# Message arithmetic in place in PSUM, with ScalarE making the bfloat16 parts, and VectorE taking them early in the step

## The chip, the cores and the metric

The kernel runs on one core of a Trainium2 chip. The metric is the device time of one execution in microseconds (us). The engines are named as in the profile: PE is TensorE's matmul, PEld its weight load, DVE is VectorE, ACT is ScalarE, POOL is GpSimd, SP is SyncE. Each engine works through its own instructions in order, and semaphores hold an instruction until what it needs from another engine is done.

## The reference

A message-passing layer on a random graph with 12,500 nodes and 800,000 edges: messages are made per edge and summed per destination node.

```python
N, deg, D, De = 12500, 64, 64, max(16, 1)
E = N * deg
...
m_in = jnp.concatenate([x[src], x[dst], e_attr], axis=-1)
msg = _silu(m_in @ w_msg)
agg = _segment_sum(msg, dst, N)
return _silu(jnp.concatenate([x, agg], axis=-1) @ w_upd)
```

All tensors are float32. `src` and `dst` are random, so edges have to be brought into the order of their destinations first.

## The kernel before

Nodes are cut into buckets of 98 (`BK`). The kernel runs two pipelines in one loop.

The first sorts the edges. A step (`Step`) takes eight columns of 128 edges: `onehot` makes, on ACT, a one-hot row of the bucket for each edge (eight Square instructions at L378, one Relu over all at L379); `sums` adds these up on DVE (L387 to L392, the first slice copied by ACT at L385); `count` forms counts on PE (L405 to L408); `ranks` reduces them on DVE (L413); `expand` writes the records to the places of their ranks (L422 to L426, DVE); `move` gathers them into the buckets with PE (L441), and ACT copies a finished chunk out of PSUM (L445). `place` computes new write pointers (L458, L459) and `scatter` writes the chunk to a store in HBM with an indirect DMA, issued by POOL (L463).

The second works through the sorted store. A group (`Group`) forms over several steps (`fourth`, `middle`, `fifth`) and loads 64 tiles of 128 edges; a batch (`Batch`) is eight of these tiles. `gather` fetches the source nodes' rows with eight indirect DMAs on POOL (L623). `onehot` makes q, the one-hot of the destination within the bucket, on DVE (L628), and ACT copies the edge features beside it (L629). `transpose` turns q with PE (L637), and ACT copies the result to qt (L640), after copying the weights w (L616). `product` multiplies qt with the weights into the PSUM bank pre (L646). `message` adds the gathered rows (DVE, L652) and applies Silu (ACT, L653). `parts` splits the float32 message into three bfloat16 parts by two subtractions (DVE, L661): the upper half of each float32 word is the part, and the rest goes on to the next. `reduce` multiplies the parts with q's one-hot (PE, L672), and `add` sums the parts (L685) and adds them to the accumulator (L687).

The tiles of a bucket come in units of one, two and, for most of the run, four (`QU`); only batches with units of four are split into parts, the others go through a float32 matmul (L674).

`period` writes out by hand the order in which one round of both pipelines is issued. In it h is the step that is new, z the one before, p and s older ones; q is the batch that is new, t the one before, a the one before that, and r the oldest. The order on each engine is that of the calls. PSUM banks, like pre, tq and z, have one buffer each; messages have two, gathered rows three, the buckets' one-hots (hf) three.

Of the kernel before, what the change touches and what calls it, by code (L numbers as in the profile page):

```python
# [17 lines left out]
D = 64  # L18
# [26 lines left out]
def mpnn_kernel(tc, x, e_attr, src, dst, w_msg, w_upd, out):  # L45
# [22 lines left out]
    with es:  # L68
# [294 lines left out]
        class Step:  # L363
# [10 lines left out]
            def onehot(c):  # L374
                c.hf = hp.tile([P, M, NBK], F32, name="hf")

                for k in range(M):
                    nc.scalar.activation(c.hf[:, k, :], iof, AF.Square, bias=c.hi[:, k:k + 1])  # L378
                nc.scalar.activation(c.hf, c.hf, AF.Relu, bias=ones, scale=-1.0)  # L379
# [216 lines left out]
        class Batch:  # L596
# [51 lines left out]
            def message(t):  # L648
                w = t.n * D
                t.msg = mp.tile([P, 3, BT * D], F32, name="msg")  # L650
                u_ = t.msg[:, 2, :]
                nc.vector.tensor_tensor(out=u_[:, 0:w], in0=t.pre[:, 0:w], in1=t.g.rearrange("p a b -> p (a b)")[:, 0:w], op=OP.add)  # L652
                nc.scalar.activation(t.msg[:, 0, 0:w], u_[:, 0:w], AF.Silu)  # L653

            def parts(t):

                t.split = t.grp.u == QU
                if t.split:
                    up = t.msg.bitcast(BF16).rearrange("p k (f two) -> p k f two", two=2)
                    for k in range(2):  # L660
                        nc.vector.tensor_tensor(out=t.msg[:, k + 1, :], in0=t.msg[:, k, :], in1=up[:, k, :, 1], op=OP.subtract)  # L661

            def reduce(t):
                t.ag = pag.tile([P, 512], F32, name="ag")
                w = 3 * D
                if t.split:
                    q = t.q.bitcast(BF16).rearrange("p i (k two) -> p i k two", two=2)[:, :, 0:BK, 1]
                    m = t.msg.bitcast(BF16).rearrange("p k (f two) -> p k f two", two=2)[:, :, :, 1]
                for i in range(t.n):
                    u, k = i // t.grp.u, i % t.grp.u  # L670
                    if t.split:
                        nc.tensor.matmul(t.ag[0:BK, u * w:(u + 1) * w].rearrange("p (k d) -> p k d", d=D), q[:, i, :], m[:, :, i * D:(i + 1) * D], start=(k == 0), stop=(k == t.grp.u - 1))  # L672
                    else:
                        nc.tensor.matmul(t.ag[0:BK, u * D:(u + 1) * D], t.q[:, i, 0:BK], t.msg[:, 0, i * D:(i + 1) * D], start=(k == 0), stop=(k == t.grp.u - 1))  # L674
# [17 lines left out]
        def period(step=None, batch=None, ptr_new=None):  # L692
# [12 lines left out]
            if h:  # L705
                h.onehot()
            if q:
                q.onehot()
            for g in forms:
                g.fourth()  # L710
# [26 lines left out]
            if a:  # L737
# [399 lines left out]
```

## Time and profile before

| | us |
|---|---|
| median of 3 runs | 9224.63 |
| lowest and highest | 9221.28, 9232.15 |
| the profiled execution | 9227.92 |
| its span | 9226.0 |

| engine | busy us | share of the span |
|---|---|---|
| PE | 8209.7 | 89% |
| PEld | 5889.5 | 64% |
| DVE | 8201.5 | 89% |
| ACT | 5087.3 | 55% |
| POOL | 6721.0 | 73% |

A group's row in the profile gives line, engine, operation, output and inputs by the program's names, shapes and count, then the busy time in us with the mean of one in ns, then the engine's idle time just before these instructions, and what ended it. A row of the timeline gives start and duration in us, engine, line, operation, names, and a count if several are merged. Durations of neighbours on one engine overlap a little, so the distance between two starts is what an instruction costs its queue. An issue of an indirect DMA counts as POOL's busy time; the fixed pause between two of them is listed as idle.

### The profile page before, as it was taken

The page shows a single profiled execution, that of the slowest core. Times are in us where ns is not written, and L with a number is a line of the kernel's source. Part 1 is how long each engine was busy: PE and PEld are TensorE (multiplying, and loading weights), DVE is VectorE, ACT ScalarE, POOL GpSimd, SP SyncE. Part 2 cuts the span into 40 slices and gives each one's busy share as a digit, 9 for nine tenths or more (in the row PEclk, how much of TensorE's full clock was granted, in tenths as well). Part 3 has the DMA queues.
Part 4 walks back from the last instruction along what each step waited for, and adds up shares of the span by engine and source line. Part 5 has one row for each costly group of instructions (what it writes and reads, how often), then busy time and mean ns, then how long its engine had stood idle before and what let it go on. Part 6 is the DMA issues. An engine that isn't in the chain of part 4 may idle for free. (4 is left out here: it accounts for less than half of the span.)

```text
span 9226.0 us, 146657 instructions
## 1 busy us (share of the span) xinstructions
PE 8209.7 (89%) x44136; PEld 5889.5 (64%) x44897; DVE 8201.5 (89%) x17559; ACT 5087.3 (55%) x12546; POOL 6721.0 (73%) x6868
## 2 busy tenths in 40 slices
PE   8999999898888889988888889888888888888777
PEld 4677766666666666666666666666666666666676
DVE  6999999999999999999999999999999999999332
ACT  5555556555555555555555555555555555555222
POOL 1566667777777777777777777777777777777776
PEclk9999999999999999999999999999999999999666
DMA  2222222222222222222222222222222222222333
GB/s 58 48 53 53 53 53 58 55 49 53 52 56 50 55 51 53 53 53 55 52 50 53 55 50 55 55 50 56 51 54 54 50 56 49 56 54 48 55 50 50
DMA packets 651770, 487.53 MB, mean 53 GB/s; under 512 B 475175, under 2 KB 522727, under 8 KB 650967
## 3 DMA queue, kind: packets, MB, share of 16 engines
q0 software_dynamic: 235968, 344.76, 16.8%
q1 hardware_dynamic: 412295, 132.58, 6.8%
q8 instruction: 361, 5.91, 0.3%
q14 instruction: 442, 3.62, 0.1%
q10 hardware_dynamic: 2704, 0.66, 0.1%
HBM read 330.05 MB, written 147.34 MB: 52 GB/s over the span
## 5 line engine op out<-in xcount | busy, mean ns | idle before, releaser
L623 POOL DMA_INDIRECT g<-A_d,sidx x6322 | 6182.9, 978 | 2084.3 <-issue 1561.6
L441 PE MATMUL pl<-X,hf 128*128 128x223 f32 (+5 forms) x12504 | 4191.7, 485 | 0.0
L441 PEld LDWEIGHTS pl<-X,hf 128*128 128x128 f32 x12504 | 2292.3, 190 | 1347.6 <-issue 1026.6
L426 DVE TENSOR_TENSOR X<-cb,rec 128x442 f32<-128x442 f32 (+5 forms) x3126 | 2710.3, 929 | 27.1
L378 ACT ACTIVATE hf<-iof,shi 128x128 f32<-128x128 f32 x6256 | 1910.9, 389 | 1364.8 <-PE pl L441 1361.5
L646 PEld LDWEIGHTS pre<-w,qt 114*128 114x128 f32 x10368 | 1266.3, 193 | 330.0 <-issue 313.9
L646 PE MATMUL pre<-w,qt 114*128 114x64 f32 x10368 | 1241.2, 273 | 52.0 <-DVE msg L652 49.0
L653 ACT ACTIVATE msg<-msg 128x512 f32<-128x512 f32 (+1 forms) x818 | 501.4, 613 | 1205.9 <-DVE msg L652 1202.1
L413 DVE TENSOR_REDUCE rank<-z 128x8 f32<-128x1024 f32 x782 | 950.4, 1215 | 71.0 <-PE z L408 41.4
L652 DVE TENSOR_TENSOR msg<-pre,g 128x512 f32<-128x512 f32 (+1 forms) x818 | 546.5, 668 | 492.8 <-DMA g<-A_d,sidx 348.3
L640 ACT ACTIVATE qt<-tq 114x1024 f32<-114x1024 f32 (+1 forms) x818 | 800.9, 979 | 327.6 <-PE tq L637 326.9
L406 PE MATMUL z<-G,onesb 128*128 128x384 bf16 x1564 | 515.8, 330 | 475.2 <-DVE G L387 428.6
L661 DVE TENSOR_TENSOR msg<-msg 128x512 f32<-128x512 f32 x1296 | 893.0, 689 | 22.6
L379 ACT ACTIVATE hf<-hf,ones 128x1024 f32<-128x1024 f32 x782 | 898.7, 1149 | 25.4
L637 PE MATMUL tq<-ident,q 128*114 128x128 f32 x6322 | 886.9, 286 | 14.7 <-ACT nodes L185 13.3
L637 PEld LDWEIGHTS tq<-ident,q 128*114 128x114 f32 x6322 | 781.9, 142 | 141.2 <-ACT nodes L185 21.2
L672 PE MATMUL ag<-msg,q 128*98 128x192 bf16 x5184 | 570.7, 252 | 290.5 <-DVE msg L661 111.5
L445 ACT ACTIVATE blk<-pl 128x512 f32<-128x512 f32 x521 | 309.0, 593 | 931.2 <-PE pl L441 923.3
L628 DVE TENSOR_TENSOR q<-cb,lo 128x784 f32<-128x784 f32 (+1 forms) x818 | 769.0, 940 | 0.6
L463 POOL DMA_INDIRECT st<-blk,ptrs x520 | 519.7, 999 | 338.4 <-issue 133.8
L672 PEld LDWEIGHTS <-q 128*98 128x98 bf16 x5184 | 488.6, 126 | 376.6 <-issue 324.9
L646 PEld LDWEIGHTS pre<-BW,qt 114*128 114x128 f32 x2276 | 331.7, 225 | 150.6 <-issue 149.9
(145 smaller groups left out, 6673.2 us busy)
## 6 DMA issues: line engine op xcount, KB each, us to landing
g<-A_d,sidx POOLq DMA_INDIRECT x6322
ea<-in_e_attr SPq DMA_DIRECT2D x260, 192.0 KB
rt<-st SPq DMA_DIRECT2D x1296, 34.0 KB
st<-blk,ptrs POOLq DMA_INDIRECT x520
rt<-st SPq DMA_DIRECT2D x498, 8.5 KB
nodes<-in_x SPq DMA_DIRECT2D x62, 98.0 KB
rt<-st SPq DMA_DIRECT2D x320, 17.0 KB
A_d<-nodes SPq DMA_DIRECT2D x32, 98.0 KB
```

Source lines behind the costliest of these rows:

```text
L378: nc.scalar.activation(c.hf[:, k, :], iof, AF.Square, bias=c.hi[:, k:k + 1])
L379: nc.scalar.activation(c.hf, c.hf, AF.Relu, bias=ones, scale=-1.0)
L413: nc.vector.tensor_reduce(out=c.rank, in_=c.z, axis=AX.X, op=OP.max)
L426: nc.vector.tensor_tensor(out=c.x[:, k:k + 2, 2:2 + n * R].rearrange("p k (s c) -> p k s c", c=R), in0=hit[:, k:k + 2, 0:n, None].to_broad ...
L441: nc.tensor.matmul(pl[:, 0:w], c.hf[:, k, :], c.x[:, k, 0:w], start=False, stop=(n == C - 1))
L623: nc.gpsimd.indirect_dma_start(out=t.g[:, i, :], out_offset=None, in_=A_d, in_offset=bass.IndirectOffsetOnAxis(ap=t.grp.sidx[:, k:k + 1], ...
L628: nc.vector.tensor_tensor(out=t.q[:, 0:n, 0:BK], in0=ioB[:, None, 0:BK].to_broadcast([P, n, BK]), in1=t.grp.lo[:, i0:i0 + n, None].to_broa ...
L637: nc.tensor.transpose(t.tq[0:KQ, j * P:(j + 1) * P], t.q[:, j, :], ident)
L640: nc.scalar.activation(t.qt[:, 0:w], t.tq[0:KQ, 0:w], AF.Copy)
L646: nc.tensor.matmul(t.pre[:, i * D:(i + 1) * D], t.qt[:, i * P:(i + 1) * P], w, start=True, stop=True)
L661: nc.vector.tensor_tensor(out=t.msg[:, k + 1, :], in0=t.msg[:, k, :], in1=up[:, k, :, 1], op=OP.subtract)
L672: nc.tensor.matmul(t.ag[0:BK, u * w:(u + 1) * w].rearrange("p (k d) -> p k d", d=D), q[:, i, :], m[:, :, i * D:(i + 1) * D], start=(k == 0 ...
```

## The change

A split message stays in the PSUM bank in which its product was made. DVE adds the gathered rows there, in place; ACT applies Silu there, in place, and then copies the result to a bfloat16 tile in SBUF: the first part. DVE subtracts that part from the message in PSUM, in place; ACT copies the remainder to bfloat16: the second part. DVE's second subtraction writes the third part, bfloat16, directly. The bank is free for the next product only after that. Messages that aren't split get their sum in place too, and Silu writes them to a float32 tile. The parts now lie contiguous, where they were every other bfloat16 of a float32 tile.

In `period`, the sum and Silu of batch a come before the ranks of step z, both subtractions come in the first half of the step, around the one-hot of batch q, and the eight Squares of step h are split in two halves around them. `fourth` of the forming groups moves behind the second subtraction, and `add` behind `expand`.

```diff
-            def onehot(c):
-                c.hf = hp.tile([P, M, NBK], F32, name="hf")
-
-                for k in range(M):
+            def onehot(c, part=None):
+
+                if part != 1:
+                    c.hf = hp.tile([P, M, NBK], F32, name="hf")
+
+                for k in range(0 if part != 1 else ZB, M if part != 0 else ZB):
                     nc.scalar.activation(c.hf[:, k, :], iof, AF.Square, bias=c.hi[:, k:k + 1])
-                nc.scalar.activation(c.hf, c.hf, AF.Relu, bias=ones, scale=-1.0)
+                if part != 0:
+                    nc.scalar.activation(c.hf, c.hf, AF.Relu, bias=ones, scale=-1.0)
...
             def message(t):
                 w = t.n * D
-                t.msg = mp.tile([P, 3, BT * D], F32, name="msg")
-                u_ = t.msg[:, 2, :]
-                nc.vector.tensor_tensor(out=u_[:, 0:w], in0=t.pre[:, 0:w], in1=t.g.rearrange("p a b -> p (a b)")[:, 0:w], op=OP.add)
-                nc.scalar.activation(t.msg[:, 0, 0:w], u_[:, 0:w], AF.Silu)
-
-            def parts(t):
-
                 t.split = t.grp.u == QU
+                pre = t.pre[:, 0:w]
+                nc.vector.tensor_tensor(out=pre, in0=pre, in1=t.g.rearrange("p a b -> p (a b)")[:, 0:w], op=OP.add)
                 if t.split:
-                    up = t.msg.bitcast(BF16).rearrange("p k (f two) -> p k f two", two=2)
-                    for k in range(2):
-                        nc.vector.tensor_tensor(out=t.msg[:, k + 1, :], in0=t.msg[:, k, :], in1=up[:, k, :, 1], op=OP.subtract)
+                    t.msg = mp.tile([P, 3, BT * D], BF16, name="msg")
+                    nc.scalar.activation(pre, pre, AF.Silu)
+                    nc.scalar.activation(t.msg[:, 0, 0:w], pre, AF.Copy)
+                else:
+                    t.msg = mp.tile([P, BT * D], F32, name="m32")
+                    nc.scalar.activation(t.msg[:, 0:w], pre, AF.Silu)
+
+            def part(t, k):
+
+                if t.split:
+                    nc.vector.tensor_tensor(out=t.pre if k == 1 else t.msg[:, k, :], in0=t.pre, in1=t.msg[:, k - 1, :], op=OP.subtract)
+                    if k == 1:
+                        nc.scalar.activation(t.msg[:, k, :], t.pre, AF.Copy)
...
@@ period
             if q:
                 q.gather(BT // 2, BT)
-            if h:
-                h.onehot()
-            if q:
-                q.onehot()
-            for g in forms:
-                g.fourth()
             if z:
                 z.count()
             if t:
...
                 t.transpose(1)
             if r:
                 r.reduce()
+            if a:
+                a.message()
             if z:
                 z.ranks()
+            if h:
+                h.onehot(0)
             if a:
-                a.message()
+                a.part(1)
+            if q:
+                q.onehot()
+            if h:
+                h.onehot(1)
+            if a:
+                a.part(2)
+            for g in forms:
+                g.fourth()
+            if z:
+                z.expand()
             if r:
                 r.add()
-            if z:
-                z.expand()
             if h:
                 h.sums()
...
             if e:
                 e.place(ptr_new)
-            if a:
-                a.parts()
             for g in forms:
                 g.middle()
                 g.fifth()
```

`reduce` reads the parts as `t.msg[:, :, i * D:(i + 1) * D]` in place of the strided view.

More of the change, by code (lines that the diff above doesn't have):

```diff
@@ L671, in reduce @@
                     if t.split:
[L672 removed]
+                        nc.tensor.matmul(t.ag[0:BK, u * w:(u + 1) * w].rearrange("p (k d) -> p k d", d=D), q[:, i, :], t.msg[:, :, i * D:(i + 1) * D], start=(k == 0), stop=(k == t.grp.u - 1))
                     else:
[L674 removed]
+                        nc.tensor.matmul(t.ag[0:BK, u * D:(u + 1) * D], t.q[:, i, 0:BK], t.msg[:, i * D:(i + 1) * D], start=(k == 0), stop=(k == t.grp.u - 1))
             def add(t):
```

1 line of the change is left out of this document (removed).

## The prediction

> **What bounds the kernel now.** I read the busy times by stretch first, then each engine's groups inside the long stretch, then the timeline of single steps. Columns of the first view: busy time of PE, PEld, DVE, ACT and POOL, with instruction counts, and the granted TensorE clock.
>
> ```profile
> core 0: us, PE busy (x) PEld busy (x) DVE busy (x) ACT busy (x) POOL busy (x), PEclk, DMA share, GB/s
> 0.00:1440.00 1440.00, 1368.59 (x7045) 939.06 (x7173) 1277.13 (x3103) 842.24 (x2091) 800.60 (x842) 1.00 0.24 53
> 1440.00:8520.00 7080.00, 6334.81 (x34091) 4473.92 (x34725) 6682.20 (x13789) 4078.41 (x10137) 5408.16 (x5487) 0.99 0.23 53
> 8520.00:8700.00 180.00, 119.83 (x654) 107.30 (x654) 69.75 (x186) 43.74 (x97) 131.67 (x137) 0.64 0.29 55
> 8700.00:9226.00 526.00, 386.50 (x2352) 369.26 (x2351) 172.41 (x482) 122.94 (x223) 380.59 (x405) 0.66 0.32 51
> ```
>
> Batches that split their messages (four tiles to a bucket) run in the second stretch. Its groups on POOL and DVE:
>
> ```profile
> L623 POOL DMA_INDIRECT g<-A_d,sidx x5065 | 4986.5, 984 | 1543.5 <-issue 1223.5 <-DMA g<-A_d,sidx 215.5 <-DVE q L628 47.5
> L463 POOL DMA_INDIRECT st<-blk,ptrs x422 | 422.3, 1001 | 128.6 <-issue 115.5 <-ACT blk L445 7.9 <-ACT msg L653 2.1
> ```
>
> ```profile
> L661 DVE TENSOR_TENSOR msg<-msg 128x512 f32<-128x512 f32 x1270 | 875.1, 689 | 22.1
> L413 DVE TENSOR_REDUCE rank<-z 128x8 f32<-128x1024 f32 x634 | 769.8, 1214 | 0.0
> ...
> L652 DVE TENSOR_TENSOR msg<-pre,g 128x512 f32<-128x512 f32 x634 | 435.4, 687 | 201.9 <-issue 107.9 <-DMA g<-A_d,sidx 91.1
> ...
> L423 DVE TENSOR_TENSOR cb<-cb,rank 128x240 f32<-128x240 f32 x634 | 259.1, 409 | 0.0
> ```
>
> L413 runs once a step: 634 steps in 7080 us, 11.17 us each. POOL's two groups, busy and idle, make 4986.5+1543.5+422.3+128.6 = 7081 us: POOL issues without a break, eight gathers of 0.984+0.305 us and two thirds of a scatter per step. So POOL sets the pace, by a little: DVE's only large wait is for gathers, 201.9/634 = 0.32 us, so DVE needs 11.17-0.32 = 10.85 us a step. Whatever adds over 0.32 us to DVE's step makes DVE the bound. PE is busy 6334.81/634 = 9.99 us, ACT 6.4.
>
> **The chain that the new order closes.** Call S the end of a step's last sum on DVE (L389 or L392). PE's count of the next step waits for S, the transposes follow it, then ACT's copy to qt (L640). Three steps; columns are start, duration, engine, line:
>
> ```profile
> 5013.27 0.23 DVE L392 TENSOR_TENSOR G<-G 128x128 bf16<-128x128 bf16 x1
> ...
> 5013.44 0.94 POOL L623 DMA_INDIRECT g<-A_d,sidx  x1 [0.31 <-issue]
> 5013.59 1.03 PE L637 MATMUL tq<-ident,q 128*114 128x128 f32 x8
> ...
> 5013.80 1.41 DVE L661 TENSOR_TENSOR msg<-msg 128x512 f32<-128x512 f32 x2
> ...
> 5014.66 0.29 ACT L629 ACTIVATE q<-rt 128x128 f32<-128x128 f32 x1
> 5014.68 1.35 POOL L623 DMA_INDIRECT g<-A_d,sidx  x1 [0.30 <-issue]
> 5014.86 0.38 ACT L616 ACTIVATE w<-BW 114x64 f32 x2
> 5015.13 0.21 DVE L506 CAST sidx<-rt 128x64 int32<-128x64 f32 x1
> 5015.15 1.00 ACT L640 ACTIVATE qt<-tq 114x1024 f32<-114x1024 f32 x1
> ...
> 5015.78 0.97 DVE L628 TENSOR_TENSOR q<-cb,lo 128x784 f32<-128x784 f32 x1
> ...
> 5016.66 1.22 DVE L413 TENSOR_REDUCE rank<-z 128x8 f32<-128x1024 f32 x1
> ...
> 5017.83 0.69 DVE L652 TENSOR_TENSOR msg<-pre,g 128x512 f32<-128x512 f32 x1
> ...
> 5018.44 0.55 DVE L685 TENSOR_REDUCE sum<-ag 98x128 f32<-98x384 f32 x1
> ```
>
> ```profile
> 5023.78 0.36 DVE L389 TENSOR_TENSOR G<-G,hf 128x128 bf16<-128x128 bf16 x1
> ...
> 5024.38 1.41 DVE L661 TENSOR_TENSOR msg<-msg 128x512 f32<-128x512 f32 x2
> ...
> 5034.54 0.23 DVE L392 TENSOR_TENSOR G<-G 128x128 bf16<-128x128 bf16 x1
> 5034.68 1.41 DVE L661 TENSOR_TENSOR msg<-msg 128x512 f32<-128x512 f32 x2
> ```
>
> ```profile
> 5024.58 1.03 PE L637 MATMUL tq<-ident,q 128*114 128x128 f32 x8
> ...
> 5035.23 1.04 PE L637 MATMUL tq<-ident,q 128*114 128x128 f32 x8
> ```
>
> From S to the end of the transposes: 14.62-13.50 = 1.12, 25.61-24.14 = 1.47, 36.27-34.77 = 1.50; mean 1.36 us. Today this hurts nobody: after S, DVE does the parts of the batch before, the one-hot and the ranks, and comes to the sum (L652) 4.3 us later (5017.83 against 13.50), when qt is long copied; and between a message's Silu and its parts lie the expansion and the sums of the step, so that DVE never waits for ACT there.
>
> The changed program's queues, as built, are: DVE: sum (message), ranks, part 1, one-hot q, part 2, then expansion, add, sums. ACT: w, **copy to qt**, Silu, copy 0, four squares, copy 1, the features of q, four squares, Relu, G. PE is unchanged: count, transposes, reduction, moves, product. Queues run in order. Silu itself needs only the sum, but it stands behind the qt copy, hence behind the transposes and S; and DVE waits at part 1 with everything else of the step queued behind it: q, part 2, the expansion, the sums, and so the next S. The ring S, transposes, qt, Silu, copy, parts, expansion, next S is closed, and its length is the step.
>
> Prices on ACT, from the groups of the same stretch, and eight squares from the timeline:
>
> ```profile
> L379 ACT ACTIVATE hf<-hf,ones 128x1024 f32<-128x1024 f32 x633 | 727.6, 1149 | 20.6
> L640 ACT ACTIVATE qt<-tq 114x1024 f32<-114x1024 f32 x634 | 638.9, 1008 | 175.1 <-PE tq L637 174.9
> L653 ACT ACTIVATE msg<-msg 128x512 f32<-128x512 f32 x634 | 398.6, 629 | 1019.9 <-DVE msg L652 1019.2
> L385 ACT ACTIVATE G<-hf 128x256 bf16<-128x256 f32 x633 | 253.0, 400 | 0.0
> L445 ACT ACTIVATE blk<-pl 128x512 f32<-128x512 f32 x423 | 250.5, 592 | 670.2 <-PE pl L441 669.5
> ```
>
> ```profile
> 5011.13 2.44 ACT L378 ACTIVATE hf<-iof,shi 128x128 f32<-128x128 f32 x8 [3.08 <-PE pl L441]
> ```
>
> *First stall.* From S: transposes 1.36, qt 1.01, Silu 0.63, copy 0.59 (L445: PSUM to SBUF, the same size), about 0.04 for each of three hand-overs, less 0.09 by which one ACT instruction overlaps the next (5014.66+0.29 against 5014.86): part 1 starts at S+3.62. DVE is free earlier: 0.30, 0.24, -0.09 us from S to L661 in the three steps, mean 0.15; about 0.11 for what stands there now and then (L506 to L628 is 0.65 us, once in eight batches); the sum 0.61 and the ranks 1.17 by starts (5016.66, 5017.83, 5018.44). That is S+2.04. DVE stands 1.58 us.
>
> *Second stall.* Part 1 as L652 (one input from PSUM, 512 wide) 0.69, ending at S+4.31. Copy 1 waits for it and for four squares, 2.44/2 = 1.22 from S+3.49: it runs from 4.71 to 5.30, part 2 starts at 5.34. DVE has by then done part 1 (0.61 by starts) and q (0.88): free at 5.11. It stands 0.23 us.
>
> *The parts themselves.* Two of L661 take 5015.13-5013.80 = 1.33 by starts; two like L652 take 1.22: a gain of 0.11. Writing back into the bank that is read costs nothing extra as L423 shows: 240 elements in 409 ns, 512 in 687, the same 150 to 160 ns over 0.96 elements per ns.
>
> *Later in the step nothing waits.* ACT ends G near S+8.4 (5.30, then the features 0.29, four squares 1.22, Relu 1.15, G 0.40). DVE reaches the sums near S+10: the add, the expansion and the sums take 24.14-18.44 = 5.7 us in one of the steps shown, the sums being their last quarter, and all of it now follows part 2's end at S+5.95. PE's product waits for part 2 (S+5.95) where before it waited for the sum; only the step whose chunk ends halfway reaches it so early, and PE has 12.5-10 us to spare. ACT gets 1.2 us of copies more and has 4.8 to spare.
>
> *At nothing:* batches before 1440 us, which aren't split, so that no part follows their Silu; those after 8520 us, where DVE is 33 to 39% busy behind gathers (if that cover were gone, the few split ones there would cost 1.8 us each); and the moved fourth steps of forming groups, DVE work that only changes its place. The reduction now reads contiguous parts: whatever that gives PE disappears in PE's own idle time, which grows.
>
> The step: 10.85 - 0.11 + 1.58 + 0.23 = 12.55 us. Unknown is an ACT instruction that writes to PSUM, which no row shows. Its bounds are 0.59 (L445, the cheapest of this size) and 0.69 (L652); below that I have no row, and allow another 0.1 for Silu and the copies together. I take 0.63, Silu's own row. The other unknown is TensorE's clock:
>
> ```profile
> PE z L406 <- DVE G L387: 413.8, 397, 2.5
> ```
>
> ```profile
> 8565.17 1.96 PE L637 MATMUL tq<-ident,q 128*114 128x128 f32 x8 [0.42 <-ACT nodes L185]
> ```
>
> The clock is 0.99 where PE is busy 89% (its longest wait for S 2.5 us), and 0.64 to 0.66 at 67 to 73%, where eight transposes take 1.96 us for 1.03. PE would be busy 9.99/12.55 = 80%, with gaps of some 2.3 us before each count. Between the rows, by proportion, the clock is 0.79: 42% of the time at half speed, and 42% of the chain's 1.36 us is 0.57. The gaps are however such as the fast stretch has already; I add 0.05, and keep 0 and 0.57 as ends.
>
> The Trainium skill ("TensorE: Matmul & The Clock Gate", Part 1) says that the clock goes down to half after at least one idle window of about 3.4 us. By that rule a gap of 2.3 us never does it, and the step would be 12.55 us, the time 10,103; the trace agrees, with waits up to 2.5 us at a clock of 0.99.
>
> 12.60-11.17 = 1.43 us on 634 steps is 907; on the profiled execution's 9227.9 us (3 over the median of the runs) that is 10,135. I say 10,130.
>
> **Rivals.**
> (a) Faster, because the gathers quicken and the stalls don't come. For it: the gather that starts within L661 takes 1.35 us, the one before it 0.94; where no L661 runs the mean is 944 ns against 984:
>
> ```profile
> L623 POOL DMA_INDIRECT g<-A_d,sidx x404 | 381.2, 944 | 123.0 <-issue 116.0 <-DMA g<-A_d,sidx 5.8 <-DVE ACC L687 0.3
> ```
>
> Both new parts read one input from PSUM, as L652 does. At 950 ns, POOL's step is (5065 x 1.255 + 551)/634 = 10.9 us and the time 9228 - 0.27 x 634 = 9,055. It decides only while DVE's stalls stay under 11.17-10.74 = 0.43 us a step; against it, 1.81. Even if Silu came straight behind the sum (which ends at S+0.95), part 1 could start only at 0.95+0.63+0.59+0.12 = S+2.29 and part 2 at 2.16+1.22+0.59+0.04 = S+4.01, 0.25 and 0.23 us after DVE is free: no gain even then.
> The Trainium skill ("SBUF — State Buffer", Who interferes with whom) says that a VectorE instruction with two SBUF inputs contends with a GpSimd instruction that reads SBUF; by that rule the change gives POOL its 34 ns back, and the trace agrees (1.35 against 0.94).
> (b) Slower still: the clock drops in most steps. For it the last stretches, against it the second. With 0.57 to 1.36 us on the chain the step is 13.1 to 13.9: 10,450 to 10,960.
> (c) No change: the stall only takes the place of the wait for gathers. It would need stalls of 0.4 us: 9,230.
>
> **How the numbers follow.** My case 0.75, between 9,980 (12.35 a step: Silu and both copies at ACT's low end, no clock loss) and 10,450; (b) 0.10; a stall half as long, 9,300 to 9,950, 0.05; (c) 0.02; (a) 0.08. About 0.2% is what this kernel's measurement tells from no change. The range 9,930 to 10,520 leaves out (a), (c), most of the half stall and the upper part of (b). Faster 0.08, same 0.02, slower 0.90.
>
> **What would show it.** DVE's two subtractions idle behind ACT, about 1.6 and 0.2 us each time, some 1,150 us in all; gathers near 950 ns with POOL now idle beyond 0.3 us; no DVE wait for gathers; steps of 12.6 us; ACT's qt still waiting for the transposes. Wrong if part 1 starts without idle, or if Silu's row ends before qt's.

## The result and the profile after

| | before | after |
|---|---|---|
| median | 9225.17 us (4 runs) | 11229.12 us (4 runs, 11223.86 to 11242.6) |
| profiled span | 9226.0 us | 11232.1 us |
| granted TensorE clock, mean | 0.968 | 0.87 |

The ratio is 1.217, with an interval of 1.216 to 1.219: slower by 2,004 us. The direction was right; the time lies far above the range, whose upper end was 10,520.

Busy time of the engines by stretch, after (busy time of PE, PEld, DVE, ACT and POOL with instruction counts, then the granted clock):

```profile
core 0: us, PE busy (x) PEld busy (x) DVE busy (x) ACT busy (x) POOL busy (x), PEclk, DMA share, GB/s
0.00:1440.00 1440.00, 1277.42 (x6347) 865.72 (x6462) 1170.75 (x2812) 775.12 (x1904) 718.85 (x754) 0.97 0.22 48
2000.00:10000.00 8000.00, 6403.61 (x30484) 4481.55 (x31050) 6088.05 (x12340) 4260.49 (x10206) 4719.01 (x4914) 0.87 0.19 42
10500.00:11232.00 732.00, 555.47 (x3148) 515.23 (x3149) 266.92 (x717) 192.22 (x383) 511.58 (x543) 0.65 0.32 51
```

No engine is full in the long stretch any more: PE 80%, DVE 76%, POOL 59%, and the clock is 0.87 where it was 0.99. The first 1440 us hold 10% fewer PE instructions than before (6347 against 7045). So there, too, something takes time, although no message is split yet.

The groups of the long stretch, after. The window holds 567 steps, 14.1 us each:

```profile
L626 POOL DMA_INDIRECT g<-A_d,sidx x4536 | 4338.0, 956 | 1647.4 <-issue 1255.3 <-DVE pre L655 308.4 <-DMA g<-A_d,sidx 50.0
...
L416 DVE TENSOR_REDUCE rank<-z 128x8 f32<-128x1024 f32 x567 | 692.0, 1220 | 311.4 <-PE z L411 286.6 <-PE z L409 23.4 <-issue 0.3
...
L679 PE MATMUL ag<-msg,q 128*98 128x192 bf16 x4536 | 598.5, 288 | 673.1 <-DVE rb L572 337.4 <-DVE wl L533 335.6
L643 ACT ACTIVATE qt<-tq 114x1024 f32<-114x1024 f32 x567 | 580.7, 1024 | 3090.0 <-PE tq L640 3090.0
...
L667 DVE TENSOR_TENSOR pre<-pre,msg 128x512 f32<-128x512 f32 x567 | 396.7, 700 | 1046.9 <-ACT msg L659 1046.9
L655 DVE TENSOR_TENSOR pre<-pre,g 128x512 f32<-128x512 f32 x567 | 396.7, 700 | 210.6 <-PE pre L649 154.7 <-issue 11.8 <-PE z L411 6.4
L667 DVE TENSOR_TENSOR msg<-pre,msg 128x512 bf16<-128x512 f32 x567 | 392.2, 692 | 39.7
...
L659 ACT ACTIVATE msg<-pre 128x512 bf16<-128x512 f32 x567 | 338.6, 597 | 17.9
L658 ACT ACTIVATE pre<-pre 128x512 f32<-128x512 f32 x567 | 335.4, 592 | 3.5 <-DVE pre L655 3.4
L669 ACT ACTIVATE msg<-pre 128x512 bf16<-128x512 f32 x567 | 327.6, 578 | 0.0
```

The forecast chain is there: ACT's qt copy stands behind the transposes (3090 us of idle), Silu and copy 0 behind the qt copy, and DVE's first subtraction behind copy 0: 1046.9/567 = 1.85 us a step. The second stall is small, 39.7/567 = 0.07.

What was not forecast is in the row of L679, the reduction. PE waits 673 us there, half for DVE's L533 and half for L572. The same group in the kernel before, 634 steps:

```profile
L672 PE MATMUL ag<-msg,q 128*98 128x192 bf16 x5072 | 552.1, 250 | 290.4 <-DVE msg L661 111.5 <-DVE rb L569 103.5 <-DVE wl L530 72.5
```

Both lines (L530 and L569 there) belong to the fourth steps of a forming group: they read the group's own products out of PSUM, and these products take turns with the batches' reduction in **one** PSUM buffer (a pool of one, with one tag). The pool, the reduction's tile and the group's first and second product:

```python
pag = pool("pag", 1, space=PSUM)
...
t.ag = pag.tile([P, 512], F32, name="ag")
...
g.ps = pag.tile([P, 512], F32, name="ps1", tag="ag")
...
g.ps = pag.tile([P, 512], F32, name="ps2", tag="ag")
```

Two neighbouring forming steps of after on the timeline, first PE, then DVE:

```profile
5048.74 1.91 PE L640 MATMUL tq<-ident,q 128*114 128x128 f32 x8
5055.38 1.44 PE L679 MATMUL ag<-msg,q 128*98 128x192 bf16 x8 [4.73 <-DVE wl L533]
5056.61 5.00 PE L444 MATMUL pl<-X,hf 128*128 128x461 f32 x8
5061.45 1.90 PE L649 MATMUL pre<-w,qt 114*128 114x64 f32 x16
...
5065.94 0.32 PE L409 MATMUL z<-G,onesb 128*128 128x384 bf16 x1 [0.17 <-issue]
...
5072.50 1.44 PE L679 MATMUL ag<-msg,q 128*98 128x192 bf16 x8 [4.75 <-DVE rb L572]
```

```profile
5054.50 0.69 DVE L667 TENSOR_TENSOR msg<-pre,msg 128x512 bf16<-128x512 f32 x1
5055.11 0.15 DVE L532 TENSOR_TENSOR wl<-ps,wl 128x1 f32<-128x1 f32 x1
5055.18 0.15 DVE L533 TENSOR_SCALAR wl<-ps 128x1 f32<-128x1 f32 x1
...
5062.67 0.23 DVE L395 TENSOR_TENSOR G<-G 128x128 bf16<-128x128 bf16 x1
...
5066.91 1.22 DVE L416 TENSOR_REDUCE rank<-z 128x8 f32<-128x1024 f32 x1 [2.83 <-PE z L411]
```

The transposes end at 5050.65. The reduction starts at 5055.38, right after L533 (5055.18 + 0.15), and L533 now stands behind part 2. PE's queue is in order: the moves, the product and the next step's count all come late with it. DVE has its last sum ready at 5062.90, but the count starts only at 5065.94, and the ranks wait 2.83 us.

Step lengths, taken from the trace as distances of successive starts of the ranks (L416), sorted by whether the step runs L536 (first product read) or L571 (second):

| after, 2000 to 10000 us | steps | mean us |
|---|---|---|
| neither | 354 | 13.10 |
| with L536 | 71 | 17.61 |
| with L571 | 70 | 17.04 |
| the step after it | 71 | 12.67 |

In the kernel before all four classes lie between 10.97 and 11.25 us (1500 to 8500 us).

Over the whole run, from the first split message to the last ranks, the step is 14.09 us for 11.16: 634 x 2.937 = 1,862 us. The stretch before the first split message takes 1,591 us for 1,441, and the tail after the last ranks 706 us for 713.

### The profile page after: what moved, and what is told of

Its sections match the earlier page's. It is cut to its first block, busy times and chain, and to the rows that moved or that the text cites. A ratio compares the mean times of both kernels' runs of the same rounds, so it can differ in the third digit from the quotient of the medians.

```text
span 11232.1 us, 147578 instructions
## 1 busy us (share of the span) xinstructions
PE 9100.6 (81%) x44136; PEld 6467.2 (58%) x44897; DVE 8332.7 (74%) x17559; ACT 5789.2 (52%) x13842; POOL 6580.3 (59%) x6868
## 4 chain that ended last, share of the span: by engine, by line
PE 39%; DVE 28%; ACT 23%; issue 6%; POOL 2%; DMA 1%; SPq 0%; DVEq 0%; ACTq 0%; POOLq 0%
PE pl L444 15%; DVE X L429 13%; PE tq L640 7%; ACT hf L380 7%; ACT qt L643 6%; PE z L409 4%; PE pre L649 4%; ACT msg L659 3%; DVE G L390 3%; DVE msg L667 3%; ACT pre L658 3%; ACT msg L669 3%; PE z L411 3%; PE ag L679 2%; DVE ACC L694 2%
## 5 line engine op out<-in xcount | busy, mean ns | idle before, releaser
L626 POOL DMA_INDIRECT g<-A_d,sidx x6322 | 6039.9, 955 | 2477.6 <-issue 1740.2
L444 PE MATMUL pl<-X,hf 128*128 128x223 f32 (+5 forms) x12504 | 4568.7, 519 | 0.0
L444 PEld LDWEIGHTS pl<-X,hf 128*128 128x128 f32 x12504 | 2506.8, 208 | 1639.2 <-issue 1311.9
L667 DVE TENSOR_TENSOR pre<-pre,msg 128x512 f32<-128x512 f32 x648 | 453.4, 700 | 1225.8 <-ACT msg L659 1225.8
L679 PE MATMUL ag<-msg,q 128*98 128x192 bf16 x5184 | 686.9, 289 | 768.2 <-DVE rb L572 385.6
L416 DVE TENSOR_REDUCE rank<-z 128x8 f32<-128x1024 f32 x782 | 954.6, 1221 | 467.8 <-PE z L411 403.3
L640 PE MATMUL tq<-ident,q 128*114 128x128 f32 x6322 | 1081.6, 328 | 14.5 <-ACT nodes L185 12.9
L679 PEld LDWEIGHTS <-q 128*98 128x98 bf16 x5184 | 621.7, 154 | 796.8 <-issue 795.8
L640 PEld LDWEIGHTS tq<-ident,q 128*114 128x114 f32 x6322 | 967.2, 167 | 192.7 <-issue 86.8
L655 DVE TENSOR_TENSOR pre<-pre,g 128x512 f32<-128x512 f32 (+1 forms) x818 | 557.5, 681 | 458.8 <-PE pre L649 244.8
L448 ACT ACTIVATE blk<-pl 128x512 f32<-128x512 f32 x521 | 305.2, 586 | 775.9 <-PE pl L444 765.4
L409 PEld LDWEIGHTS <-onesb 128*128 128x128 bf16 x1564 | 166.6, 107 | 877.0 <-DVE G L390 730.5
L411 PE MATMUL z<-G,onesb 128*128 128x512 bf16 x1042 | 485.0, 465 | 0.0
```

Source lines behind the costliest of these rows:

```text
L409: nc.tensor.matmul(c.z[:, k + 1:k + ZB, :], onesb, c.G[:, a, 0:ZB - 1, :], start=False, stop=first)
L411: nc.tensor.matmul(c.z[:, k:k + ZB, :], onesb, c.before(a)[:, None, :].to_broadcast([P, ZB, NBK]), start=False, stop=True)
L416: nc.vector.tensor_reduce(out=c.rank, in_=c.z, axis=AX.X, op=OP.max)
L444: nc.tensor.matmul(pl[:, 0:w], c.hf[:, k, :], c.x[:, k, 0:w], start=False, stop=(n == C - 1))
L626: nc.gpsimd.indirect_dma_start(out=t.g[:, i, :], out_offset=None, in_=A_d, in_offset=bass.IndirectOffsetOnAxis(ap=t.grp.sidx[:, k:k + 1], ...
L640: nc.tensor.transpose(t.tq[0:KQ, j * P:(j + 1) * P], t.q[:, j, :], ident)
```

## The experiments

Two theories were set against each other. A: the moved fourth steps hold the one PSUM buffer and so the reduction. B, its rival: no step in particular, but TensorE's clock; the ring is as forecast, and PE's idle times in it halve the clock, which stretches PE's part of the ring further.

The runs went to several chips. On the chip of the f runs the kernel before takes 9,224 us, as in the result; on the five others it takes 11,875 to 12,031 us itself, so the e, g, h, k and m runs are read only by their ratio to it, or against each other on one chip. All edits are to the changed kernel unless said.

**The first four, on one chip where the kernel before took 11,900 us (one run each).** The first puts the fourth steps back, the second takes Silu ahead of the qt copy, the third issues eight idle matmuls (their results are overwritten by the count) ahead of each count to keep PE busy, the fourth is the first and third together:

```diff
+            for g in forms:
+                g.fourth()
             if z:
                 z.count()
...
                 a.part(2)
-            for g in forms:
-                g.fourth()
```

```diff
                 t.weights()
-                t.transpose(1)
...
                 a.message()
+            if t:
+                t.transpose(1)
```

```diff
+                    for _ in range(8 if a == 0 else 0):
+                        nc.tensor.matmul(c.z[:, k:k + ZB, :], w1, hb[:, k:k + ZB, :], start=True, stop=True)
                     nc.tensor.matmul(c.z[:, k:k + ZB, :], w1, hb[:, k:k + ZB, :], start=True, stop=False)
```

> The changed kernel with one part undone: the fourth steps of forming groups stand at the head of the step again, ahead of the sum. In the changed kernel 2 of 8 steps, those in which a group's second and third stage runs, take 17.3 us against 13.1 for a plain one. Theory A (the moved fourth step holds PE's reduction, which needs the one PSUM bank that the group's products share with it): these 158 steps fall to a plain step's length, 158 x 4.2 = 660 us less, 10,560 us, and the reduction's wait for DVE (4.7 us each) is under 2 us. Theory B (TensorE's clock alone makes the excess over the forecast, the waits only coincide with it): under 100 us less, 11,130 us or more.

> The changed kernel with ACT's copy to qt moved behind Silu and copy 0 of the message. Theory A (the ring through the transposes and qt sets the plain step): DVE's wait at part 1, 1.85 us a step on average, falls to about 0.3; the 476 plain steps lose some 1.5 us each, the forming ones little; 10,500 us. Theory C (the PSUM bank of the message, held until part 2, sets the step by holding PE's product): part 2 comes hardly earlier for PE because qt is later, 11,100 us.

> The changed kernel with eight more matmuls ahead of each count, into the bank that the count then overwrites: they fill PE's wait for the sums, and compute nothing that is used. Theory A: the granted clock rises from 0.87 to 0.93 or more, plain steps go from 13.1 to 12.5 us, forming steps stay over 16.5; 10,900 us. Theory B (clock alone): forming steps come down as well, 10,200 us. If the clock costs nothing: 11,230 us or more.

> The changed kernel with the fourth steps at the head of the step again and eight more matmuls ahead of each count. Theory A: both terms that the forecast lacked are gone, and what is left is its own sum, 12.5 to 12.6 us a step, 10,100 us within 100, at a clock of 0.95 or more. Theory B: 10,200 as without the move, so no less than the run with the added matmuls alone.

Measured: 11,338, 11,955, 12,868 and 12,058 us, clocks 0.875, 0.848, 0.887 and 0.91. The numbers expected were made for a chip like the result's and can't be held against these. Within the chip: with the extra matmuls in both, putting the fourth steps back takes off 12,868 - 12,058 = 810 us. The extra matmuls raise the clock (0.875 to 0.91) and cost 720 us all the same. The reduction's waits in the second and the first, groups of PE from 2000 to 8000 us:

```profile
L679 PE MATMUL ag<-msg,q 128*98 128x192 bf16 x3296 | 454.3, 292 | 502.0 <-DVE wl L533 224.5 <-DVE rb L572 142.0 <-issue 101.4
```

```profile
L679 PE MATMUL ag<-msg,q 128*98 128x192 bf16 x3536 | 435.8, 272 | 57.5 <-issue 33.7 <-DVE wl L533 22.1 <-DVE rb L572 0.4
```

366 us against 22. The two kernels differ in Silu's place as well, so these rows agree with A but do not isolate the fourth steps; f1 below does, against the changed kernel itself.

**The same question on the result's kind of chip (f runs, 9,224 us before).** The first edit alone; the first two together; the first with four idle matmuls; and an order in which, besides the first two, `q.onehot` comes ahead of part 1, `add` between the two parts, and the squares after part 2:

```diff
                 z.ranks()
-            if h:
-                h.onehot(0)
-            if a:
-                a.part(1)
             if q:
                 q.onehot()
-            if h:
-                h.onehot(1)
+            if a:
+                a.part(1)
+            if r:
+                r.add()
             if a:
                 a.part(2)
-            for g in forms:
-                g.fourth()
+            if h:
+                h.onehot()
             if z:
                 z.expand()
-            if r:
-                r.add()
```

> The changed kernel with one part undone: the fourth steps of forming groups stand at the head of the step again, ahead of the sum. Theory A (the moved fourth step holds PE's reduction): the forming steps (17.3 us against 13.1 for a plain one) fall to a plain step's length, 10,560 us, ratio to the kernel before 1.145; the reduction's wait for DVE is under 2 us. Theory B (TensorE's clock alone makes the excess over the forecast): 11,130 us or more, 1.206. An earlier run of this kernel was on a chip on which the kernel before took 11,900 us, so that its time could not be read.

> The changed arithmetic in another order: fourth steps at the head; on ACT Silu and copy 0 ahead of the copy to qt, all eight squares behind copy 1; on DVE sum, ranks, one-hot q, part 1, add, part 2, expansion, sums. If ring and forming steps are all that the changed kernel loses (theory A): DVE waits nowhere for ACT, its step is 10.75 us and POOL's 10.9 sets the pace: 9,060 us, ratio 0.982, gathers 955 ns, clock 0.97 or more. Theory C (holding the PSUM bank until part 2 costs by itself): PE's product waits for part 2, 9,600 us or more.

> The changed kernel with the fourth steps at the head and ACT's copy to qt behind Silu and copy 0; the squares stay between the copies. Theory A: DVE waits 0.25 us at part 1 and 0.25 at part 2, a step is 11.2 us, 9,250 us, ratio 1.003. Theory C: 9,700 us or more.

> The changed kernel with the fourth steps at the head and four more matmuls ahead of each count, into the bank that the count overwrites (they compute nothing that is used), against PE's wait for the sums. Theory A: what is left is the forecast's own sum, 12.5 to 12.7 us a step, 10,100 us within 100, ratio 1.095, clock 0.95 or more. If the clock costs nothing, no less than the run with the fourth steps alone.

| kernel | median us | ratio to before | clock | split step us |
|---|---|---|---|---|
| before | 9,224 | | 0.968 | 11.16 |
| after | 11,229 | 1.217 [1.216, 1.219] | 0.87 | 14.09 |
| f1, fourth steps back | 10,309 | 1.118 [1.115, 1.121] | 0.914 | 12.88 |
| f4, and four idle matmuls | 10,291 | 1.116 [1.111, 1.121] | 0.944 | 12.64 |
| f3, fourth back and Silu first | 9,985 | 1.083 [1.080, 1.086] | 0.926 | 12.37 |
| f2, the other order | 9,281 | 1.006 [1.004, 1.009] | 0.937 | 11.27 |

*f1* is the run that decides. Moving one call back to the head of the step takes off 920 us, and B left no such gain; A had expected 670, since it counted no gain ahead of the split stretch. (It is not quite the old place: in the kernel before, the fourth steps follow the parts and the one-hot q on DVE; here those come later, so that the fourth steps stand earlier than they ever did.) Its groups from 2000 to 8400 us (497 steps):

```profile
L416 DVE TENSOR_REDUCE rank<-z 128x8 f32<-128x1024 f32 x497 | 605.0, 1217 | 67.9 <-PE z L411 62.6 <-PE z L409 4.1
...
L679 PE MATMUL ag<-msg,q 128*98 128x192 bf16 x3976 | 464.0, 266 | 0.0
...
L655 DVE TENSOR_TENSOR pre<-pre,g 128x512 f32<-128x512 f32 x497 | 347.7, 699 | 65.5 <-issue 12.3 <-DMA g<-A_d,sidx 11.4 <-PE z L411 5.3
L667 DVE TENSOR_TENSOR pre<-pre,msg 128x512 f32<-128x512 f32 x496 | 347.0, 700 | 780.2 <-ACT msg L659 780.2
L667 DVE TENSOR_TENSOR msg<-pre,msg 128x512 bf16<-128x512 f32 x496 | 343.1, 692 | 34.9
```

The reduction's wait is gone (673.1 to 0.0), the ranks' wait falls from 311.4/567 = 0.55 to 67.9/497 = 0.14 us, and what remains is the forecast ring: 780.2/496 = 1.57 us before part 1. Sorted as above, over 2000 to 8400 us, the steps of f1 take 13.00 us (neither), 12.36 (with L536), 13.13 (with L571) and 12.60 (the one after): the excess of the forming steps is gone, and the others hardly change. Of the 920 us, 1.217 x 634 = 771 (a step of 12.876 us for 14.093) are in the split stretch and 148 ahead of it: the first split message comes at 1,443 us again. There the same buffer is shared by the unsplit reduction, L681; its row in the first 1600 us of after:

```profile
L681 PE MATMUL ag<-m,q 128*98 128x64 f32 x1408 | 146.6, 256 | 101.7 <-DVE wl L533 61.2 <-DVE rb L572 40.5
```

In f1 it has 0.1 us of idle in the first 1440 us. The held buffer need not be all of the 771: the fourth steps' own DVE work is 0.18 us a step, 113 us in all, and in f1 it can be covered by the stall before part 1. How much of it is was not measured.

*f4* tells the clock's share in what remains. Stretches from 2000 to 8400 us of f1 and of f4, in the columns above:

```profile
2000.00:8400.00 6400.00, 5453.00 (x27198) 3760.60 (x27197) 5317.63 (x10804) 3713.81 (x8936) 4143.88 (x4304) 0.92 0.18 46
```

```profile
2000.00:8400.00 6400.00, 5786.42 (x29672) 3823.64 (x29669) 5400.85 (x10982) 3778.49 (x9092) 4211.27 (x4377) 0.96 0.18 47
```

Half of the missing clock comes back, and the split step is 0.24 us shorter. The eight transposes take 1.07 us in the mean for 1.36 in f1, and the wait before part 1 falls to 1.30 us:

```profile
L669 DVE TENSOR_TENSOR pre<-pre,msg 128x512 f32<-128x512 f32 x505 | 353.3, 700 | 657.7 <-ACT msg L661 657.7
```

But the added matmuls cost about 110 us ahead of the split stretch, and the whole is the same within its spread (10,271 and 10,310). So 0.04 of the clock, less what the added matmuls take of PE's time, was worth 0.24 us a step in this one trace; the expected 10,100 was missed.

*f3* was expected near 9,250, and missed. With Silu ahead of the qt copy part 1 hardly waits, but part 2 does:

```profile
L667 DVE TENSOR_TENSOR pre<-pre,msg 128x512 f32<-128x512 f32 x485 | 338.6, 698 | 68.4 <-ACT msg L659 66.9
L667 DVE TENSOR_TENSOR msg<-pre,msg 128x512 bf16<-128x512 f32 x484 | 334.7, 692 | 528.4 <-ACT msg L669 528.4
```

528.4/484 = 1.09 us. ACT's timeline in f3 says why:

```profile
6008.06 0.58 ACT L658 ACTIVATE pre<-pre 128x512 f32<-128x512 f32 x1 [4.84 <-DVE pre L655]
6008.67 0.60 ACT L659 ACTIVATE msg<-pre 128x512 bf16<-128x512 f32 x1
6009.17 1.02 ACT L643 ACTIVATE qt<-tq 114x1024 f32<-114x1024 f32 x1
6010.07 1.27 ACT L380 ACTIVATE hf<-iof,shi 128x128 f32<-128x128 f32 x4
6011.24 0.58 ACT L669 ACTIVATE msg<-pre 128x512 bf16<-128x512 f32 x1
```

The qt copy and four squares now stand between copy 0 and copy 1, and the wait has moved from the first part to the second.

*f2* takes that away, too. Its groups from 2000 to 8000 us:

```profile
L667 DVE TENSOR_TENSOR pre<-pre,msg 128x512 f32<-128x512 f32 x532 | 366.9, 690 | 0.0
L667 DVE TENSOR_TENSOR msg<-pre,msg 128x512 bf16<-128x512 f32 x533 | 363.8, 683 | 0.1
```

```profile
L626 POOL DMA_INDIRECT g<-A_d,sidx x4261 | 4045.8, 949 | 1298.2 <-issue 1044.4 <-DMA g<-A_d,sidx 140.5 <-DVE msg L667 39.9
L466 POOL DMA_INDIRECT st<-blk,ptrs x355 | 372.8, 1050 | 283.1 <-ACT blk L448 208.5 <-issue 39.3 <-ACT w L619 29.5
```

DVE waits for neither part, and POOL sets the pace again: its four numbers make 5,999.9 us of 6,000. The gathers have become quicker, 8 x (984 - 949) = 0.28 us a step, but the scatter's idle time, most of it for ACT's copy of the chunk (L448), is 283.1/532 = 0.53 us a step for 0.20 before. The one eats up the other: 9,281 us where 9,060 had been expected. So the arithmetic in PSUM, ACT's copies and this order together cost 0.6% over the kernel before; the other 11,229 - 9,281 = 1,948 us of the loss go with the order. What the arithmetic costs in the old order was not run. Which of f2's moves beyond f3's brings how much of the 704 us between them was not taken apart.

**Two more cross-checks, on the slower chips.** `reduce` (with `add`) behind the first moves while `fourth` stays late (the moves' call, and with it ACT's copy of a finished chunk, comes ahead of the sums for that): if the held buffer matters only because the moves and the product queue behind the reduction, the forming steps should lose their excess. And the kernel before with `fourth` behind its message, the late fourth step without the new ring:

```diff
-            if r:
-                r.reduce()
...
+            if p:
+                e = p.move(0)
             if r:
+                r.reduce()
                 r.add()
             if h:
                 h.sums()
-            if p:
-                e = p.move(0)
```

```diff
             if a:
                 a.message()
+            for g in forms:
+                g.fourth()
             if r:
                 r.add()
```

The second diff is to the kernel before. A third kernel, order2, is f2 with all squares at the head of the step, ahead of `fourth`, to let the chunk's copy come earlier on ACT.

> The order of the earlier run (Silu and copy 0 ahead of qt, fourth steps at the head, add between the parts) with all eight squares moved to the head of the step on ACT, where ACT stood 2.5 us a step before Silu; Relu stays behind copy 1. That run's PE waited for ACT's copy of a finished chunk, which stood behind the squares (L441, 246 us in 6400). Theory A (that wait is what kept it at 11.28 us a step): it goes under 60 us, the step falls to POOL's 10.9 us, 9,060 us, ratio 0.982, clock 0.97. Theory C (holding the message's bank costs by itself): PE still waits, 9,230 us or more.

> The changed kernel with the fourth steps where the change put them, but PE's reduction behind the moves, so that a reduction that waits for them holds fewer others up. Theory A (what costs is PE's queue behind the waiting reduction): forming steps come down from 17.3 us to under 14, 10,450 us, ratio 1.135. Rival (what costs is DVE's own work in the moved fourth steps, or the clock): forming steps stay over 16 us, 11,100 us or more.

> The kernel before with one part of the change alone: the fourth steps stand behind the sum of the message on DVE, ahead of add. Theory A: the reduction of 2 of 8 steps waits some 3 us longer; PE has 1.2 us a step to spare, so a part of it shows: 9,400 to 9,900 us, ratio 1.02 to 1.07, with the waits on PE's reduction over 300 us in all. Rival (the place costs only together with the ring): 9,230 us.

> The order of the earlier run (Silu and copy 0 ahead of qt, fourth steps at the head, add between the parts) with all eight squares at the head of the step on ACT. Run before on a chip on which the kernel before took 11,995 us: ratio 0.980 there, but not readable for this chip's limits. Theory A (PE's wait for ACT's copy of a finished chunk kept the earlier order at 11.28 us a step): that wait goes under 60 us in 6400, the step falls to POOL's 10.9 us, 9,060 us, ratio 0.982, clock 0.97. Theory C (holding the message's bank until part 2 costs by itself): PE's product waits for part 2, 9,230 us or more.

> The changed kernel with the fourth steps where the change put them, but PE's reduction behind the moves. Theory A (what costs is PE's queue behind the waiting reduction): forming steps come down from 17.3 us to under 14, 10,450 us, ratio 1.135. Rival (DVE's own work in the moved fourth steps, or the clock): forming steps stay over 16 us, 11,100 us or more.

> The kernel before with one part of the change alone: the fourth steps stand behind the sum of the message on DVE, ahead of add. Theory A: the reduction of 2 of 8 steps waits some 3 us longer; PE has 1.2 us a step to spare, so a part of it shows: 9,300 to 9,900 us, ratio 1.01 to 1.07, the waits on PE's reduction over 300 us in all. Rival (the place costs only together with the ring): 9,230 us.

> The changed kernel with the fourth steps where the change put them, but PE's reduction behind the moves. Theory A (what costs is PE's queue behind the waiting reduction): forming steps come down from 17.3 us to under 14, 10,450 us, ratio 1.135. Rival (DVE's own work in the moved fourth steps, or the clock): forming steps stay over 16 us, 11,100 us or more. Two runs of it on chips on which the kernel before took 12,000 us gave ratios of 1.03, with PE's results reaching the other engines late.

> Silu and copy 0 ahead of qt, fourth steps at the head, add between the parts, all eight squares at the head of the step on ACT. Theory A: PE's wait for ACT's copy of a finished chunk (L441) goes under 60 us in 6400, the step falls to POOL's 10.9 us, 9,060 us, ratio 0.982. Theory C (holding the message's bank until part 2 costs by itself): PE's product waits for part 2, 9,230 us or more.

> The changed kernel with the fourth steps where the change put them, but PE's reduction behind the moves. Theory A (what costs is PE's queue behind the waiting reduction): forming steps come down from 17.3 us to under 14, 10,450 us, ratio 1.135. Rival (DVE's own work in the moved fourth steps, or the clock): forming steps stay over 16 us, 11,100 us or more. On a chip on which the kernel before takes about 12,000 us: ratio 1.02 to 1.03, as three times before.

> Silu and copy 0 ahead of qt, fourth steps at the head, add between the parts, all eight squares at the head of the step on ACT. Theory A: PE's wait for ACT's copy of a finished chunk (L441) goes under 60 us in 6400, the step falls to POOL's 10.9 us, 9,060 us, ratio 0.982. Theory C (holding the message's bank until part 2 costs by itself): PE's product waits for part 2, 9,230 us or more. On a chip on which the kernel before takes about 12,000 us: ratio 0.97 to 0.98, as three times before.

| kernel | ratio to before, one chip each |
|---|---|
| reduce late | 1.028 [1.022, 1.034], 1.027 [1.019, 1.034], 1.020 [1.013, 1.026], 1.020 [1.011, 1.029] |
| before with fourth late | 1.007 [1.005, 1.010], 1.009 [1.005, 1.012] |
| order2 | 0.980 [0.975, 0.985], 0.978 [0.972, 0.984], 0.974 [0.969, 0.979], 0.972 [0.966, 0.978] |

None of the four chips was like the result's, so no absolute time could be tested, and the changed kernel itself was not run on them. What can be read on these chips is the shape of the steps. With the reduction late (g2), a group's forming steps and the one after take 16.80 + 13.41 + 15.88 us (2000 to 10000 us), 2.0 more than three plain steps of 14.68; in e2, fourth late and the reduction early, 7.4 more than three of its plain ones (16.54 + 16.24 + 15.30 against 13.57 each), in e1, fourth back, 0.3 less. That speaks for A, but the expectation was missed: one of the two forming steps stays at 16.80 us, where under 14 had been expected (for a chip like the result's), the plain step is 1.1 us longer than in e2, and the whole takes 2 to 3% more than the kernel before, where e2 took 0.5% more.

The kernel before with a late fourth step lost less than the 1 to 7% expected. Its reduction waits 176 us in 6000 for these two lines, where more than 300 in the whole run were expected:

```profile
L672 PE MATMUL ag<-msg,q 128*98 128x192 bf16 x3296 | 434.2, 279 | 309.2 <-DVE wl L530 102.2 <-issue 87.0 <-DVE rb L569 73.6
```

So on these chips a late fourth step alone costs little; the large price needs the new order around it. In it the two stalled parts stand ahead of the fourth step, as the rows of after show; that this alone makes the difference was not tested.

Order2 takes 2 to 3% less than the kernel before, but on the slower chips alone, where f1's edit took less as well (e1, 0.953, from one run of each kernel). On a chip like the result's it was not run, so whether it beats the kernel before there is open.

## Why the prediction was right or wrong

**The step that failed** stands under *At nothing*: "and the moved fourth steps of forming groups, DVE work that only changes its place". Its own work was indeed unchanged. What was left out is who waits for it: the fourth step frees a PSUM buffer that PE's reduction needs, and PE's moves, product and next count queue behind the reduction. The rows were there: the kernel before had PE waiting 103.5 and 72.5 us for the two lines, with waits of up to 1.9 us. Before, the fourth step came behind the one-hot q, which ends at S + 3.25 us in the step that the prediction shows (5015.78 + 0.97 against 13.50); now it comes behind part 2, which the forecast itself puts at S + 5.95. Measured cost: 920 us, by f1, which leaves 10,309 of the 11,229, a time inside the stated range.

**Batches before 1440 us at nothing**: wrong by 150 us, and for the same reason; 148 of them go with the fourth steps. That no part follows an unsplit Silu was true and beside the point.

**The ring**: right in place, as f1 shows it alone; first stall 1.57 us (forecast 1.58), second 0.07 (0.23). That the first stall agrees to 0.01 is luck. In f1, by the means of its steps from 2000 to 8400 us, the transposes end at S + 2.10 us (forecast 1.36) and part 1 starts at S + 4.32 (3.62), but DVE has ended its ranks only at S + 2.75 (2.04): two terms are 0.7 us too short each, and the difference hides it. The 1.36 came from three steps; over the split stretch of the kernel before the mean is 1.58. Of the other 0.52, 0.29 is the transposes' own duration (1.36 us for 1.07), which goes with the clock (below). On DVE's side the waits before the sum and the ranks and the fourth steps at the head make 0.46 of the 0.71. The order of the queues, the qt copy behind the transposes, no lasting wait for gathers at the sum (11.4 us in 497 steps): as forecast. The 0.32 us of that wait in the kernel before is all of the row's idle time; the row puts 91.1 of the 201.9 us to gathers and names no releaser for 107.9. In after itself the first stall is 1.85, since the count comes late there.

**The prices**: ACT's Silu in place in PSUM takes 592 ns (0.63 taken), the copies 597 and 578 (0.59), DVE's subtractions 700 and 692 (0.69). Copies and subtractions are within 12 ns of these, Silu is 37 ns below its SBUF row. POOL stands idle now, as forecast: the gathers wait 308 us for the sum that frees their buffer.

**The remainder of the ring's step**: f1 has 12.88 us where the forecast had 12.60; x 634 that is 178 us, all of the distance from 10,130 to 10,309. By DVE's own numbers: it is busy 5317.63/497 = 10.70 us a step, where before it was 6682.20/634 = 10.54. The forecast had it fall by 0.11, so this term is off by 0.27. The forecast counted by starts, in which neighbours overlap by about 0.09; an instruction that comes after idle time overlaps with none. That accounts for it: with the durations of all DVE instructions added up one by one, a step is 11.65 us in the kernel before and 11.66 in f1, so what has gone is overlap. The waits before the sum and the ranks, 0.13 and 0.14 us, come where nothing was forecast, and the stalls are 0.17 shorter.

**The clock**: mis-sized. The step took the gaps to be "such as the fast stretch has already" and added 0.05 us. PE's waits for S in f1 are shorter than the forecast's 2.3 us (652.4/471 = 1.39 in the mean), and the clock is half for part of the time all the same, 0.92 for 0.99. By f4, 0.04 of the clock goes with 0.24 us a step and 0.27 us of the first stall. How the late count divides was not measured further. Rival (b) as the sole cause falls: e4 against e1 and f4 against f1 have the higher clock and gain nothing in all (their added matmuls cost time, too), while f1 gains 920 us, almost all of it in the forming steps.

**Rival (a)**: its mechanism is right and its condition not met, as the text had it. The gathers take 956 ns in after and 949 in f2 (forecast 950), but DVE's stalls decide. The remark that even Silu straight behind the sum would bring no gain fits f3 (1.083); the stall it put at part 2, 0.23 us, is 1.09, because the remark left out the qt copy, which then stands between ACT's two copies beside the squares. Rival (c) is out.

**The tail** at nothing: right, 706 us for 713.

## What to carry to other kernels

Before a step is moved and priced at nothing, look up which buffer it frees, who on another engine waits for that buffer, and what is queued behind the waiter; a row with a small wait in the profile of before (here 72.5 and 103.5 us) is the pointer to it. A ring of two engines can be priced by adding up its instructions from rows, but where its ends lie in the step is to be taken as a mean over many steps, not from three; to shorten it, both of its waits must be followed, since taking one away (f3) can move it to the next. And a change that bundles new arithmetic with a new order is taken apart first: here the arithmetic with another order (f2) ends 0.6% above the kernel before, and the rest of the loss goes with the order.

## What the runs showed of the hardware

**The clock falls without a long wait.** Waits of PE in f1 from 2000 to 8400 us (total, times, longest):

```profile
PE z L409 <- DVE G L390: 652.4, 471, 3.0
PE pl L441 <- ACT blk L448: 119.2, 166, 0.8
```

No other wait in that stretch is longer than 1.7 us, and the granted clock is 0.92; in the kernel before the longest wait for S is 2.5 us at 0.99. Nor does the longest wait alone decide: in f2 no wait of PE from 2000 to 8000 us is longer than 1.7 us, and the clock is 0.95. In f1 PE is busy for 46% (median) of the last 3.41 us, the trace's shortest spell, ahead of each of the 240 spells at half speed in that stretch. The Trainium skill ("TensorE: Matmul & The Clock Gate", Part 1) says that the clock goes to half after at least one idle window of about 3.4 us. The trace doesn't agree in the length: here waits of up to 3.0 us were enough for part of the time to pass at half speed.

**The gathers and the subtractions did contend.** With one input of each subtraction in PSUM, a gather takes 949 to 960 ns in after, f1 and f2, where it took 984. Gathers that start within L661 took 1.17 us in the mean (452 of them); those that start within the first subtraction of f1 take 0.94 (406). That agrees with the Trainium skill ("SBUF — State Buffer", Who interferes with whom), by which a VectorE instruction with two SBUF inputs contends with GpSimd's reads.

**On some chips PE's results reach ACT late, by the records.** From the kernel before with a late fourth step, on one of the slower chips:

```profile
6015.90 1.04 PE L637 MATMUL tq<-ident,q 128*114 128x128 f32 x8
...
6018.85 0.38 ACT L616 ACTIVATE w<-BW 114x64 f32 x2
...
6022.08 1.02 ACT L640 ACTIVATE qt<-tq 114x1024 f32<-114x1024 f32 x1 [2.85 <-remote]
```

The transposes end by the records at 6016.94, ACT is free at 6019.23, and the copy that needs nothing else starts at 6022.08. On the result's kind of chip the same hand-over takes 0.04 us (f1 and after). Durations of single instructions are the same on both kinds, as the 1.04 and 1.02 us here. The cause is open, and so is whether the results come late or the records put PE's ends too early.
